# The last batch's gate values stored as rows in the tail, weight loads behind the first two gathers, and gate gathers ahead of the last token gathers

## The chip, the cores and the metric

The kernel runs on 1 core of one Trainium2 chip. The metric is the device time of one execution in microseconds (us). Before the change three executions took 1396.22 to 1399.36 us, with a median of 1397.73 us. One more execution was profiled; all rows below come from it.

## The reference

The program is an attention without softmax whose output is multiplied by `u`, followed by a mixture of experts with a capacity. B = 8, S = 2496, D = 256, 8 experts, capacity 80:

```python
scores = (1.0 / S) * np.matmul(z, z.transpose(0, 2, 1))
x = u * np.matmul(np.maximum(scores, 0.0) ** 2, v)      # rows of all batches: N = 19968
logits = x @ w_gate
expert_idx = np.argmax(logits, axis=1)
gate_w = softmax(logits)[expert_idx]                    # of the chosen expert
out = zeros((N, D))
for e in range(E):
    tok_idx = tokens of expert e, at most `capacity` of them (largest gate_w)
    h = np.maximum(x[tok_idx] @ w1[e], 0.0)             # 256 -> 1024
    out[tok_idx] = gate_w[tok_idx, None] * (h @ w2[e])  # 1024 -> 256
```

## The kernel before

**Main part.** Eight batches with five column chunks of 512 each (the last has 448) go through TensorE (PE): scores, square, attention, then a chunk of `x` is made, stored in the DRAM tensor `xs` (one row a token), and multiplied with the gate's weights. After each batch the logits become gate values, one column of `gall` per 128 tokens. For the batches up to the seventh these values go to the DRAM tensor `gd` by `gate_store` (L651): PE transposes the columns, VectorE (DVE) copies the result, SyncE (SP) writes rows of 512 bytes. For the last batch they go by `gate_put` (L661): SP writes straight from `gall` with a swapped access pattern, which makes every value a piece of 4 bytes. The last batch is done in two parts, 16 columns (four chunks) in `finished_late` and 4 columns in `ahead`.

**Tail.** `ahead` (L1616) computes the 8 experts, one unit of 80 tokens each. All engines have their order written out by hand there, so an engine does its instructions in the order of the program, and what waits holds up all that stands behind it on that engine. The steps of a unit i:

- `token(i)` (L1471): DVE finds the row numbers `tok` of the unit's tokens, GpSimd (POOL) gathers these rows of `xs` into `xg` by an indirect DMA.
- `whole(i)`: DVE turns `xg` into `xf`; `ffn_x`, `ffn_xl`: PE transposes it, ScalarE (ACT) and DVE make a high and a low part of it (`xTh`, `xTl`).
- `ffn1(i, part)`: PE, 6 matmuls into `hp`, ACT applies the Relu; `ffn_h(i, half)`: PE transposes `h` (`tp`), ACT and DVE split it into `hTh` and `hTl`; `ffn2(i)`: PE, 24 matmuls into `op`.
- `target(i)` (L1491): POOL gathers the gate values `gt` from `gd`, DVE works out the output rows `slo`; `result(i)`: ACT multiplies `op` by `gt` into `ob`, POOL scatters `ob` to `out`.

For the units 2 to 7 the row numbers come from tables for all of them at once: `many_blocks`, `many_rows`, `many_within` on DVE, `many_pe` and `many_fetch` on PE and ACT.

**Weights.** Each expert's w1 and w2 come as 4 pieces of 512 KB (`loads`, L774; SP issues them) into 6 places, and `split(n)` turns n of them into a high part (ACT) and a low part (DVE) and asks for one further piece each. Experts 0 and 1 are done in the main part; expert 2 is loaded whole, and its low parts are made by `half_lo` in the tail. `loads(n, after)` lets POOL write one element of each place first (L754), so that the load comes behind what POOL does before it.

Of the kernel before, what the change touches and what calls it, by code (L numbers as in the profile page):

```python
# [8 lines left out]
F32 = mybir.dt.float32  # L9
# [3 lines left out]
U16 = mybir.dt.uint16  # L13
AF = mybir.ActivationFunctionType
ALU = mybir.AluOpType
AX = mybir.AxisListType
# [3 lines left out]
P = 128  # L20
# [6 lines left out]
def attn_moe_kernel(ctx, tc, zT, uT, v, wg, w1, w2, out, seq, cap):  # L27
# [5 lines left out]
    nc = tc.nc  # L33
    V = nc.vector
# [588 lines left out]
    def gate_near(b, q0):  # L623

        _, d, ex, near = gate_t[b, q0]
        ci = n_gates[0]
        n_gates[0] += 1
        V.tensor_scalar(out=near, in0=d, scalar1=-2.0 ** -25, scalar2=0.0, op0=ALU.is_gt,
                        op1=ALU.add, accum_out=nsum[:, ci:ci + 1])
        V.scalar_tensor_tensor(out=ex, in0=ex, scalar=1.0, in1=near, op0=ALU.min, op1=ALU.max)  # L630
# [27 lines left out]
        V.tensor_copy(out=gs[:nt], in_=gt[:nt, :P])  # L658
        nc.sync.dma_start(out=gd[col:col + nt], in_=gs[:nt])

    def gate_put(b, q0):  # L661

        col, nt = gcol.pop((b, q0))
        nc.sync.dma_start(out=gd[col:col + nt].rearrange("c p -> p c"), in_=gall[:, col:col + nt])


    def count(k0, k1):
        n = (k1 - k0) * E
        tp = ps_m.tile([P, CH], F32, tag="m", name=f"tp_{k0}")
# [103 lines left out]
    def loads(n, after=None):  # L773
        n = min(n, NR - len(ready))  # L774
        for p in pieces[:n]:
            ready.append((p, load_raw(*p, after)))
        del pieces[:n]
# [11 lines left out]
    def half_lo(eng=V):  # L789
        rv, hv, lv = halves.pop(0)  # L790
        eng.tensor_tensor(out=lv, in0=rv, in1=hv, op=ALU.subtract)
# [74 lines left out]
    SPLITS = dict(zip([(qb, 0), (qb, 2), (qb, 5), (qb, 8), (qz, 2), (qz, 4), (qz, 7), (qz, 9)], early))  # L866

    RAW = {(qz, 0): (2, 1), (qz, 5): (2, 2)}
    WARM = 6
    steps = [(b, qc, r) for b in range(B) for qc in range(NQ) for r in range(NP)]  # L870
    ET = mybir.EngineType
    v_raw, z_raw, w_raw = {}, {}, {}
# [60 lines left out]
    def finished_late(b, qc, r):  # L933

        kb = b * BPB
        part = kb, kb + BPB - 2
        if r == 0:
            chunk_store(b, qc)
        elif r == 1:
            chunk_hi(b, qc)  # L940
            chunk_rest(b, qc)
        elif r == 2:
            chunk_mid(b, qc)
        elif r == 3:
            chunk_lo(b, qc)
            chunk_store2(b, qc)
        elif r == 4:
            chunk_logits(b, qc)
            chunk_sum(b, qc)
        elif r == 5:  # L950
            gate_top(b, 0, NQ - 1)
        elif r == 6:
            gate(b, 0, NQ - 1)
        elif r == 7:
            gate_put(b, 0)
        elif r == 8:
            count(*part)
            up_to(*part)
            half()
# [9 lines left out]
    if True:  # L969
# [41 lines left out]
        def whole(i):  # L1011
            begin(i)
            middle(i)
            low(i)
            turn(i)
# [140 lines left out]
        for kk, c in ((3, 0), (2, 0), (3, 1), (1, 0), (2, 1), (1, 1)):  # L1156
            attend(*prev, NT - kk, [c])
            if kk == 1:
                chunk_x_last(*prev, c)
        loads(2)  # L1160
        halves_hi(2)
        chunk_logits_last(*prev)
        chunk_rows_last(*prev)
# [176 lines left out]
    def steps_of(own, tl, tw, ps_t, ps_h):  # L1340
# [64 lines left out]
        def many_blocks():  # L1405
            rk = rank[:, 0, es].rearrange("p (e o) -> p e o", o=1).broadcast_to([P, E - 2, NBLK])
            tt(le_g[1][:, :, 1:], incl[:, es], rk, ALU.is_le)
            V.tensor_reduce(out=small["cnt"][:, es], in_=le_g[1][:, :, 1:], axis=AX.X, op=ALU.add)
            bo = tl.tile([P, E - 2, NBLK], F32, name="bo_rest")
            tt(bo, le_g[1][:, :, :NBLK], le_g[1][:, :, 1:], ALU.subtract)  # L1410
            x_t["bo"] = bo

        def many_rows():
            le = le_g[1][:, :, 1:]
# [58 lines left out]
        def token(i):  # L1473

            ns = num(i)
            _, _, wr, rin, base = sl[i]
            lw = tw.tile([P, 2 * P], BF16, tag="lw", name=f"lw_{i}{own}", bufs=1)
            j = col("j", i)
            V.tensor_scalar(out=lw[:ns], in0=wr[:ns], scalar1=rin[:ns], scalar2=0.0,
                            op0=ALU.is_le, op1=ALU.add, accum_out=j[:ns])  # L1480
            tok = col("tok", i, I32)
            ts(tok[:ns], j[:ns], base[:ns], ALU.add, float(NTOK - 1), ALU.min)
            xg = tw.tile([P, 2, D], U16, tag="xg", name=f"xg_{i}{own}", bufs=8)
            nc.gpsimd.indirect_dma_start(  # L1484
                out=xg[:ns].rearrange("p h w -> p (h w)"), out_offset=None,
                in_=xs.rearrange("(n h) w -> n (h w)", h=2),
                in_offset=bass.IndirectOffsetOnAxis(ap=tok[:ns], axis=0))
            xg_t[i] = [xg, tok, j]
# [86 lines left out]
        def result(i):  # L1575
            ns, op = num(i), o_t.pop(i)
            _, gt, slo = xg_t.pop(i)
            ob = tw.tile([P, D], F32, tag="ob", name=f"ob_{i}{own}")
            nc.scalar.activation(out=ob[:ns], in_=op[:ns, :D], func=AF.Copy,
                                 scale=gt[:ns])  # L1580
            nc.gpsimd.indirect_dma_start(  # L1581
                out=out[:, :], out_offset=bass.IndirectOffsetOnAxis(ap=slo[:ns], axis=0),
                in_=ob[:ns], in_offset=None, bounds_check=NTOK - 1, oob_is_err=False)
# [6 lines left out]
        def flags_end():  # L1590
            flags2(ps_t, "t")

        early_steps = (ps_t, ps_h, places_, one_block, one_within, (many_blocks, many_rows, many_within,
                       many_pe, many_fetch), pe_block, pe_fetch, warm_up, flags_v, flags_end, x_t, sl)
        return early_steps, (empty, block, fetch, within, token, target, whole, ffn_x, ffn_xl, ffn1,
                             ffn_h, ffn2, result)
# [25 lines left out]
    def ahead(early_steps, steps):  # L1622

        ET = mybir.EngineType
        (ps_t, ps_h, places_, one_block, one_within, many, pe_block, pe_fetch, warm_up,
         flags_v, flags_end, x_t, sl) = early_steps
        many_blocks, many_rows, many_within, many_pe, many_fetch = many
        empty, _, _, _, token, target, whole, ffn_x, ffn_xl, ffn1, ffn_h, ffn2, result = steps

        def split(n):  # L1630

            for _ in range(n):
                if ready:
                    p, raw = ready.pop(0)
                    split_w(*p, raw, V)
                    loads(1)

        def spread(i):
            if i < NU:
                whole(i)  # L1640

        def from_table(i):
            pe_fetch(i)
            sl[i][2] = x_t.pop(i)

        PL = nc.gpsimd
        with tc.manual_schedule(engines={ET.Pool}):
            places_()
            one_block(0)
            pe_block(0)  # L1650
            one_block(1)
            pe_block(1)
            tot_last(B * BPB - 2, B * BPB)
            from_table(0)
            one_within(0)
            token(0)
            from_table(1)
            one_within(1)
            token(1)
            halves_hi(2)  # L1660
            for e in range(2, E, 2):
                pe_tables(e, ps_h, "h")
            gate_near(B - 1, NQ - 1)
            gcol[B - 1, NQ - 1] = gate_sum(B - 1, NQ - 1, NQ)
            gate_put(B - 1, NQ - 1)
            loads(2, PL)
            warm_up(WARM)
            many_blocks()
            whole(0)
            ffn_x(0)  # L1670
            many_rows()
            ffn_xl(0)
            many_within()
            many_pe()
            whole(1)
            ffn1(0, 0)
            many_fetch()
            ffn_x(1)
            ffn_xl(1)
            token(2)  # L1680
            token(3)
            ffn1(0, 1)
            ffn_h(0, 0)
            ffn1(1, 0)
            ffn_h(0, 1)
            empty()
            whole(2)
            ffn_x(2)
            ffn_xl(2)
            for _ in range(4):  # L1690
                half_lo()
            ffn1(1, 1)
            target(0)
            split(1)
            token(4)
            spread(3)
            split(1)
            target(1)
            ffn2(0)
            for i in range(2, NU):  # L1700
                ffn_h(i - 1, 0)
                ffn_h(i - 1, 1)
                ffn1(i, 0)
                if i + 1 < NU:
                    ffn_x(i + 1)
                    ffn_xl(i + 1)
                if i == 3:
                    result(0)
                    result(1)
                if i + 3 < NU:  # L1710
                    token(i + 3)
                split(2)
                ffn1(i, 1)
                spread(i + 2)
                split(2)
                target(i)
                if i == NU - 1:
                    ffn_h(i, 0)
                ffn2(i - 1)
                if i > 2:  # L1720
                    result(i - 1)
                if i == 5:
                    flags_v()
                if i == 6:
                    flags_end()
            ffn_h(NU - 1, 1)
            ffn2(NU - 1)
            result(NU - 1)
# [44 lines left out]
```

## Time and profile before

| what | value |
|---|---|
| median of 3 executions | 1397.73 us (1396.22 to 1399.36) |
| the profiled execution | 1396.5 us, its span 1394.8 us |
| granted TensorE clock over the span | 0.989 |
| PE busy | 1350.3 us (97%) |
| DVE, ACT busy | 1070.9 us (77%), 1027.0 us (74%) |
| POOL busy | 34.6 us (2%) |

The main part fills about 1294 us of the span and keeps PE busy nearly throughout. The change touches only the last 110 us: the end of the main part, the preparation of the tail's tables up to 1307.2 us, and the eight units from 1322.0 us on. A row of the timeline has start, duration, engine, line, operation, tiles and, in brackets, how long the engine was idle before it and what ended that. "SPq" rows are the issuing of DMAs by SP: their duration is that of the issue, not of the transfer.

### The profile page before, as it was taken

To read this page: it belongs to the slowest core of one execution; us is meant where nothing else is said; L and a number is where in the kernel's file an instruction comes from. 1 tells how busy PE (TensorE), PEld (TensorE's weight loads), DVE (VectorE), ACT (ScalarE), POOL (GpSimd) and SP (SyncE) were. 2 spreads that over 40 slices of the span, in tenths; PEclk is the share of its full clock that TensorE was granted. 3 is DMA by queue.
4 is the path that set the end of the run, shared out by engine and by line. 5 is a ranking of instruction groups with operands and counts; after the bars stand their busy time and mean duration, and the time that the engine had idled before them with its cause. 6 is when DMAs were issued, how large, how long until landed. Compare 5 with 4: busy or idle time off the path is not lost. (4 is left out here: it accounts for less than half of the span.)

```text
span 1394.8 us, 30057 instructions
## 1 busy us (share of the span) xinstructions
PE 1350.3 (97%) x12047; PEld 1128.1 (81%) x12047; DVE 1070.9 (77%) x1557; ACT 1027.0 (74%) x1322; POOL 34.6 (2%) x44
## 2 busy tenths in 40 slices
PE   8999999999999999999999999999999999999486
PEld 5888888898878888898887888888887988778365
DVE  6877787787877787877878777877877877877474
ACT  6877797777876697677876687777877778776364
POOL 0000000000000000000000000000000000000034
PEclk9999999999999999999999999999999999999699
DMA  5699969997979969997879969998789977999552
GB/s 175 195 262 282 249 183 257 244 249 211 252 188 280 244 175 248 256 268 220 234 194 261 270 156 249 260 276 209 228 230 221 278 196 219 239 288 274 149 169 85
DMA packets 262676, 318.09 MB, mean 228 GB/s; under 512 B 96558, under 2 KB 187650, under 8 KB 252290
## 3 DMA queue, kind: packets, MB, share of 16 engines
q1 hardware_dynamic: 261506, 314.79, 84.7%
q8 instruction: 96, 1.57, 0.5%
q0 software_dynamic: 1024, 1.31, 0.3%
q14 instruction: 50, 0.41, 0.1%
HBM read 153.23 MB, written 126.05 MB: 200 GB/s over the span
## 5 line engine op out<-in xcount | busy, mean ns | idle before, releaser
L441 PE MATMUL acc<-ah,vt 64*128 64x512 f32 (+1 forms) x6004 | 835.8, 387 | 1.5 <-DVE vt L159 0.9
L441 PEld LDWEIGHTS acc<-ah,vt 64*128 64x128 f32 x6004 | 606.0, 184 | 102.5 <-DVE vt L159 2.3
L441 PE MATMUL acc<-al,vt 64*128 64x512 f32 (+1 forms) x3002 | 488.3, 386 | 0.3 <-DVE al L55 0.3
L55 DVE TENSOR_TENSOR al<-a,ah 128x1024 fp32r<-128x1024 f32 (+1 forms) x240 | 291.3, 1214 | 171.3 <-ACT ah L370 130.9
L364 ACT ACTIVATE a<-s 128x512 f32<-128x512 f32 (+1 forms) x480 | 258.4, 590 | 178.2 <-PE s L361 175.7
L441 PEld LDWEIGHTS acc<-al,vt 64*128 64x128 f32 x3002 | 315.7, 184 | 51.4 <-DVE al L55 1.4
L367 ACT ACTIVATE a<-a 128x1024 f32<-128x1024 f32 (+1 forms) x240 | 253.1, 1055 | 7.4
L55 DVE TENSOR_TENSOR al<-blk,ah 128x1024 fp32r<-128x1024 f32 x160 | 193.7, 1211 | 48.8 <-PE acc L441 27.5
L342 ACT CAST ah<-blk 128x1024 fp32r<-128x1024 f32 x160 | 167.1, 1047 | 84.0 <-PE acc L441 77.7
L297 DVE STREAM_TRANSPOSE x<-a 128x512 f32<-128x512 f32 x320 | 207.5, 686 | 0.0
L370 ACT CAST ah<-a 128x1024 fp32r<-128x1024 f32 x160 | 168.0, 1050 | 5.1
L361 PE MATMUL s<-zm,zs 64*128 64x512 f32 x960 | 147.1, 394 | 1.6 <-DVE zs L121 1.2
L361 PEld LDWEIGHTS s<-zm,zs 64*128 64x128 f32 x960 | 97.4, 184 | 20.4 <-ACT a L364 1.8
L361 PE MATMUL s<-zm 64*128 64x512 f32 x480 | 74.1, 398 | 1.9 <-ACT a L364 1.9
L375 DVE CAST ah<-a 128x1024 fp32r<-128x1024 f32 (+1 forms) x80 | 53.8, 672 | 26.5 <-ACT a L367 26.3
L361 PEld LDWEIGHTS s<-zm 64*128 64x128 f32 x480 | 47.9, 184 | 11.0 <-ACT a L364 2.7
L159 DVE TENSOR_TENSOR vt<-vraw,vt 128x1024 fp32r<-128x1024 f32 (+1 forms) x40 | 46.1, 1153 | 6.9 <-ACT vt L108 6.1
L55 DVE TENSOR_TENSOR xb<-xf,xb 128x1024 bf16<-128x1024 f32 (+1 forms) x38 | 45.3, 1192 | 0.2
L55 DVE TENSOR_TENSOR xf<-xf,xb 128x1024 f32<-128x1024 f32 (+1 forms) x38 | 44.9, 1182 | 0.2
L108 ACT CAST vt<-vraw 128x1024 fp32r<-128x1024 f32 (+3 forms) x56 | 44.9, 829 | 0.0
L491 ACT CAST xb<-xf 128x1024 bf16<-128x1024 f32 (+1 forms) x39 | 39.7, 1018 | 5.0 <-DVE xf L55 2.8
L1484 POOL DMA_INDIRECT xg<-xs,tok x8 | 10.2, 1280 | 1334.0 <-DMA gd<-gall 1316.7
(173 smaller groups left out, 741.7 us busy)
## 6 DMA issues: line engine op xcount, KB each, us to landing
y<-x SPq DMA_DIRECT2D x80, 1024.0 KB, 9.1
blk<-y SPq DMA_DIRECT2D x320, 256.0 KB, 6.7
out<-idle SPq DMA_DIRECT2D x40, 512.0 KB, 3.7
vraw<-v SPq DMA_DIRECT2D x32, 512.0 KB, 7.6
zm<-zs SPq DMA_DIRECT2D x128, 128.0 KB, 6.2
ut<-uT SPq DMA_DIRECT2D x32, 512.0 KB, 6.9
xs<-xq SPq DMA_DIRECT2D x32, 512.0 KB, 7.9
wraw<-w SPq DMA_DIRECT2D x28, 512.0 KB, 6.6
```

Of the source, the lines that this page charges most:

```text
L55: V.tensor_tensor(out=o, in0=a, in1=b, op=op)
L108: eng.copy(out=o, in_=i)
L159: e1.tensor_tensor(out=vt[:, :nf, 1], in0=raw[:, :nf], in1=vt[:, :nf, 0], op=ALU.subtract)
L297: V.transpose(out=x[:, :, :, t].rearrange("p n k s -> p k n s"), in_=a)
L342: nc.scalar.copy(out=natural(ah), in_=src)
L361: nc.tensor.matmul(s, zk, zm[rows, :, y].rearrange("p h k t -> p k h t"), start=i == 0, stop=i == 2)
L364: nc.scalar.activation(out=a[:, h, :nq], in_=s[:, :nq], func=AF.Relu)
L367: nc.scalar.activation(out=a[:, :, :nq], in_=a[:, :, :nq], func=AF.Square)
L370: nc.scalar.copy(out=st["ah"][:, :, :nq], in_=a[:, :, :nq])
L375: V.tensor_copy(out=ah[:, :, :nq], in_=a[:, :, :nq])
L441: ins = nc.tensor.matmul(acc[c], vt, a[rows, k % 2, :nq], start=p == pairs[0] and group == 0 and i == 0, stop=p == pairs[-1] and group == ...
L491: nc.scalar.copy(out=xb[:, 0], in_=xf)
```

## The change

1. Both `gate_put` of the last batch go away. The 4 columns' gate values are computed later (DVE, after the first half of unit 0's `ffn_h`), and all 20 columns go to `gd` by `gate_store` there: a transpose on PE, a copy on DVE, one DMA of 20 rows of 512 bytes.
2. Of the six weight pieces that are requested before the tail's units, two instead of four are requested ahead of the last store to `xs`; four instead of two are requested behind the first two gathers.
3. `many_pe` comes ahead of `whole(0)`; the counting reduction (`many_counts`) is taken out of `many_blocks` and comes behind unit 0's transposes. WARM, the number of matmuls that only keep PE running there, is 3 instead of 6.
4. The gathers `xg` of the units 4 to 7 and the gate gathers `gt` of the units 0 to 3 are all issued before the loop over the units 2 to 7, the `gt` of 0 to 3 ahead of the `xg` of 6 and 7.
5. In the loop `result` comes one unit later and `ob` has 3 places instead of 2, `xg` 6 instead of 8.

```diff
-    def gate_put(b, q0):
-        col, nt = gcol.pop((b, q0))
-        nc.sync.dma_start(out=gd[col:col + nt].rearrange("c p -> p c"), in_=gall[:, col:col + nt])
...
-    WARM = 6
+    WARM = 3
...
             gate(b, 0, NQ - 1)
-        elif r == 7:
-            gate_put(b, 0)
...
-        loads(2)
         halves_hi(2)
         chunk_logits_last(*prev)
...
-            xg = tw.tile([P, 2, D], U16, tag="xg", name=f"xg_{i}{own}", bufs=8)
+            xg = tw.tile([P, 2, D], U16, tag="xg", name=f"xg_{i}{own}", bufs=6)
...
-            ob = tw.tile([P, D], F32, tag="ob", name=f"ob_{i}{own}")
+            ob = tw.tile([P, D], F32, tag="ob", name=f"ob_{i}{own}", bufs=3)
...
-            gate_near(B - 1, NQ - 1)
-            gcol[B - 1, NQ - 1] = gate_sum(B - 1, NQ - 1, NQ)
-            gate_put(B - 1, NQ - 1)
-            loads(2, PL)
+            loads(4, PL)
             warm_up(WARM)
             many_blocks()
+            many_pe()
             whole(0)
             ffn_x(0)
+            many_counts()
+            many_fetch()
+            ffn_xl(0)
             many_rows()
-            ffn_xl(0)
             many_within()
-            many_pe()
+            token(2)
+            ffn1(0, 0)
+            ffn1(0, 1)
             whole(1)
-            ffn1(0, 0)
-            many_fetch()
             ffn_x(1)
             ffn_xl(1)
-            token(2)
             token(3)
-            ffn1(0, 1)
             ffn_h(0, 0)
             ffn1(1, 0)
+            gate_near(B - 1, NQ - 1)
+            gcol[B - 1, 0] = gcol[B - 1, 0][0], gcol[B - 1, 0][1] + gate_sum(B - 1, NQ - 1, NQ)[1]
+            gate_store(B - 1, 0, ps_t, "t")
+            token(4)
+            token(5)
+            empty()
+            for i in range(4):
+                target(i)
             ffn_h(0, 1)
-            empty()
             whole(2)
+            half_lo()
+            half_lo()
+            ffn1(1, 1)
             ffn_x(2)
             ffn_xl(2)
-            for _ in range(4):
-                half_lo()
-            ffn1(1, 1)
-            target(0)
+            half_lo()
+            half_lo()
+            token(6)
             split(1)
-            token(4)
             spread(3)
             split(1)
-            target(1)
+            token(7)
             ffn2(0)
             for i in range(2, NU):
...
-                if i == 3:
-                    result(0)
-                    result(1)
-                if i + 3 < NU:
-                    token(i + 3)
+                if i > 2:
+                    result(i - 2)
                 split(2)
                 ffn1(i, 1)
                 spread(i + 2)
                 split(2)
-                target(i)
+                if i == 2:
+                    result(0)
+                if i > 3:
+                    target(i)
                 if i == NU - 1:
                     ffn_h(i, 0)
                 ffn2(i - 1)
-                if i > 2:
-                    result(i - 1)
+                if i == 4:
+                    flags_v()
                 if i == 5:
-                    flags_v()
-                if i == 6:
                     flags_end()
+            result(NU - 2)
             ffn_h(NU - 1, 1)
```

On SP, at the end of the main part, stand before: the two writes of gate values (`gd<-gall`), the weight pieces (`wraw`) and the two stores of the last chunk of `x` (`xs<-xq`; 128x3x512 is its first 384 tokens).

```order
L664 DMA gd<-gall 128x16x1
L756 DMA wraw_1_0_17942<-w 128x1024
L756 DMA wraw_1_1_17944<-w 128x1024
L756 DMA wraw_2_0_17968<-w 128x4x256
L756 DMA wraw_2_1_17970<-w 128x4x256
L550 DMA xs<-xq_4_17986 128x3x512
L552 DMA xs<-xq_4_17986 64x512
L664 DMA gd<-gall 128x4x1
L756 DMA wraw_1_0_18151<-w 128x1024
L756 DMA wraw_1_1_18154<-w 128x1024
```

With the change the same place of SP reads:

```order
L750 DMA wraw_1_0_17941<-w 128x1024
L750 DMA wraw_1_1_17943<-w 128x1024
L550 DMA xs<-xq_4_17981 128x3x512
L552 DMA xs<-xq_4_17981 64x512
L750 DMA wraw_2_0_18135<-w 128x4x256
L750 DMA wraw_2_1_18138<-w 128x4x256
L750 DMA wraw_1_0_18141<-w 128x1024
L750 DMA wraw_1_1_18144<-w 128x1024
L659 DMA gd<-gs_0_18262 20x128
```

Two weight pieces and both writes of single gate values no longer stand around the stores to `xs`; the pieces stand behind them, and one write of 20 rows behind those.

On POOL, from the first gather on, stand before (`xg` token rows, `gt` gate values, `out` results, the MEMSETs are those that hold back the weight loads):

```order
L1484 DMA xg_18095<-xs,tok_18093 80x512
L1484 DMA xg_18110<-xs,tok_18108 80x512
L754 MEMSET wraw_1_0_18151 128x1
L754 MEMSET wraw_1_1_18154 128x1
L1484 DMA xg_18228<-xs,tok_18226 80x512
L1484 DMA xg_18235<-xs,tok_18233 80x512
L1497 DMA gt_18293<-gd,tok_18093 80x1
L1484 DMA xg_18308<-xs,tok_18306 80x512
L1497 DMA gt_18316<-gd,tok_18108 80x1
L1484 DMA xg_18382<-xs,tok_18380 80x512
L1497 DMA gt_18414<-gd,tok_18226 80x1
L1581 DMA out<-ob_18475,slo_18295 20480x256
```

With the change POOL has, behind the first two gathers and four MEMSETs:

```order
L1477 DMA xg_18197<-xs,tok_18195 80x512
L1477 DMA xg_18230<-xs,tok_18228 80x512
L1477 DMA xg_18270<-xs,tok_18268 80x512
L1477 DMA xg_18277<-xs,tok_18275 80x512
L1490 DMA gt_18281<-gd,tok_18088 80x1
L1490 DMA gt_18285<-gd,tok_18103 80x1
L1490 DMA gt_18289<-gd,tok_18195 80x1
L1490 DMA gt_18293<-gd,tok_18228 80x1
L1477 DMA xg_18330<-xs,tok_18328 80x512
L1477 DMA xg_18349<-xs,tok_18347 80x512
L1574 DMA out<-ob_18438,slo_18283 20480x256
```

All eight `xg` now stand ahead of the first scatter to `out`; before, the `xg` of the units 6 and 7 stood behind three and four of them.

## Rows read from the trace of the kernel before

**Rows 1.** Windows over the tail: from:to, length, each engine's busy us, PEclk, DMA share, GB/s
```profile
core 0: us, PE busy (x) PEld busy (x) DVE busy (x) ACT busy (x) POOL busy (x), PEclk, DMA share, GB/s
1312.20:1319.30 7.10, 0.00 (x0) 0.00 (x0) 0.00 (x0) 0.00 (x0) 0.01 (x1) 0.50 0.00 0
...
1322.00:1342.10 20.10, 17.08 (x94) 12.62 (x95) 13.88 (x33) 9.54 (x20) 4.05 (x4) 0.82 0.23 77
1342.10:1349.00 6.90, 6.90 (x51) 5.72 (x49) 6.86 (x14) 5.93 (x12) 5.99 (x4) 1.00 0.75 233
```

**Rows 2.** Waits from 1305 us on: who waited for whom, us in total, times, longest
```profile
POOL xg L1484 <- DMA gd<-gall: 1316.7, 1, 1316.7
...
DVE xf L1508 <- DMA xg<-xs,tok: 17.4, 4, 14.8
...
ACT ob L1579 <- DMA out<-ob,slo: 2.9, 1, 2.9
```

**Rows 3.** Timeline of SP at the end of the main part
```profile
1290.64 0.62 SPq L664 DMA_DIRECT2D gd<-gall  x1
1291.36 10.01 SPq L756 DMA_DIRECT2D wraw<-w  x4
1301.46 2.42 SPq L550 DMA_DIRECT2D xs<-xq  x1
...
1306.44 0.54 SPq L664 DMA_DIRECT2D gd<-gall  x1
```

**Rows 4.** Timeline of POOL, its first gather
```profile
1319.29 1.09 POOL L1484 DMA_INDIRECT xg<-xs,tok  x1 [1316.73 <-DMA gd<-gall]
```

**Rows 5.** Timeline of ACT, the copy that the store to xs waits for
```profile
1297.67 1.93 ACT L547 COPY xq<-xp 128x1024 uint16<-128x1024 uint16 x2 [1.24 <-PE xp L545]
```

**Rows 6.** DMA issues on the page: KB each, median us from issue to landing
```profile
out<-idle SPq DMA_DIRECT2D x40, 512.0 KB, 3.7
...
xs<-xq SPq DMA_DIRECT2D x32, 512.0 KB, 7.9
```

**Rows 7.** Chain of waits near the end: start, us, what
```profile
1384.62 3.17 DMA out<-ob,slo
```

**Rows 8.** Timeline of POOL, its last scatter
```profile
1388.69 0.93 POOL L1581 DMA_INDIRECT out<-ob,slo  x1 [3.12 <-DVEq L1733]
```

**Rows 9.** Timeline of DVE, from the first row numbers to the loop
```profile
1302.52 0.21 DVE L61 TENSOR_SCALAR tok<-j,base_all 80x1 int32<-80x1 f32 x1
...
1303.91 0.17 DVE L628 TENSOR_SCALAR_CACHE_REDUCE fw<-d 128x32 f32<-128x32 f32 x1
...
1305.34 0.63 DVE L55 TENSOR_TENSOR scratch<-incl,rank 128x480 f32<-128x480 f32 x1
...
1306.57 0.65 DVE L55 TENSOR_TENSOR bo_rest<-scratch 128x480 f32<-128x480 f32 x1
1322.02 0.45 DVE L1508 COPY xf<-xg 80x512 uint16<-80x512 uint16 x1 [14.80 <-DMA xg<-xs,tok]
...
1342.08 0.88 DVE L55 TENSOR_TENSOR hTl<-tp,hTh 128x320 fp32r<-128x320 f32 x2
```

**Rows 10.** Groups of DVE instructions over the span: busy us, mean ns of one
```profile
L1479 DVE TENSOR_SCALAR_CACHE_REDUCE lw<-ws,rin_all 80x256 bf16<-80x256 bf16 x6 | 2.8, 468 | 0.0
...
L61 DVE TENSOR_SCALAR slo<-j,base_all,none 80x1 int32<-80x1 f32 x8 | 2.1, 265 | 0.0
...
L658 DVE COPY gs<-gt 20x128 f32<-20x128 f32 x7 | 1.9, 271 | 0.0
```

**Rows 11.** Timeline of PE, transposes that open a unit of the loop
```profile
1345.38 0.72 PE L1556 MATMUL tp<-ident,h 80*128 80x80 f32 x8
...
1351.99 0.72 PE L1556 MATMUL tp<-ident,h 80*128 80x80 f32 x8
...
1377.21 0.75 PE L1556 MATMUL tp<-ident,h 80*128 80x80 f32 x8
```

**Rows 12.** Windows: a stretch behind a pause of PE in the tail
```profile
1332.00:1336.00 4.00, 3.17 (x10) 2.15 (x11) 2.77 (x5) 0.36 (x2) 0.91 (x1) 0.58 0.08 21
```

More of the change, by code (lines that the diff above doesn't have):

```diff
@@ L1407, in many_blocks @@
             tt(le_g[1][:, :, 1:], incl[:, es], rk, ALU.is_le)
-            V.tensor_reduce(out=small["cnt"][:, es], in_=le_g[1][:, :, 1:], axis=AX.X, op=ALU.add)
             bo = tl.tile([P, E - 2, NBLK], F32, name="bo_rest")
@@ L1411, in many_blocks, with many_counts @@
             x_t["bo"] = bo
+        def many_counts():
+            V.tensor_reduce(out=small["cnt"][:, es], in_=le_g[1][:, :, 1:], axis=AX.X, op=ALU.add)
         def many_rows():
@@ L1591, in flags_end @@
             flags2(ps_t, "t")
-        early_steps = (ps_t, ps_h, places_, one_block, one_within, (many_blocks, many_rows, many_within,
+        early_steps = (ps_t, ps_h, places_, one_block, one_within, (many_blocks, many_counts, many_rows, many_within,
                        many_pe, many_fetch), pe_block, pe_fetch, warm_up, flags_v, flags_end, x_t, sl)
@@ L1626, in ahead @@
          flags_v, flags_end, x_t, sl) = early_steps
-        many_blocks, many_rows, many_within, many_pe, many_fetch = many
+        many_blocks, many_counts, many_rows, many_within, many_pe, many_fetch = many
         empty, _, _, _, token, target, whole, ffn_x, ffn_xl, ffn1, ffn_h, ffn2, result = steps
```

## The prediction

> **What bounds the kernel now.** I read the page first: PE is busy for 97% of the span, so the main part is PE's, and the change does not touch it. What the change touches is the tail, so I read the tail by windows, then the waits, then the timelines of SP, POOL, DVE and PE there.
>
> The windows show a hole. From 1312.2 to 1319.3 us nothing runs at all: PE, DVE and ACT are at 0.00, and the DMA share is 0.00 too [rows 1]. DVE in fact has no work from the end of its table work (1306.57 + 0.65 = 1307.2) until 1322.02, when the first gathered tokens arrive [rows 9]. The waits name what ended it: the first gather `xg` on POOL waited for the DMA `gd<-gall`, and the first `xf` waited 14.8 us for that gather [rows 2]. The gather reads `xs`, not `gd`; but SP issued the last store to `xs` at 1301.46 and the second write of gate values right behind it at 1306.44 [rows 3], and POOL started its gather only at 1319.29 [rows 4]. The store itself came late: ACT had its data ready at 1297.67 + 1.93 = 1299.6 [rows 5], but SP was still issuing four weight pieces, which took it 10.01 us behind the first write of gate values [rows 3]. So I read the hole as the work of the two writes in pieces of 4 bytes: the first slows the weight loads ahead of the store, the second is in flight together with the store and holds up its completion.
>
> From 1322.02 on there are two stages. Until the loop starts (DVE's `hTl` of unit 1 at 1342.08 [rows 9]) nothing is full: of 20.10 us DVE is busy 13.88 and PE 17.08, the latter partly at the lower clock (mean 0.82) [rows 1]. In the loop PE sets the pace at first, busy 6.90 of 6.90 us from 1342.1 on [rows 1]: the unit from 1345.38 to 1351.99 takes 6.61 us. Then three units take 1377.21 - 1351.99 = 25.22 us, 8.41 each [rows 11].
>
> **Term 1, the first gather comes earlier.** Without the first write and with two weight pieces instead of four ahead of it, SP can issue the store at 1299.6, when ACT is done. How long it then takes to land no row shows for a quiet queue. From below: SP's writes of zeros, 512 KB each to DRAM, land after 3.7 us (median); from above: the stores to `xs` in the main part, 512 KB among much other traffic, after 7.9 us [rows 6]. This store has 384 KB and a queue that is nearly empty, so I take the nearer, 3.7: landed at 1303.3. POOL starts 0.9 us behind what releases it: the last scatter at 1388.69 [rows 8], when the one before had landed at 1384.62 + 3.17 = 1387.79 [rows 7]. The gather then starts at 1304.2; its row numbers are there at 1302.52 + 0.21 = 1302.7 [rows 9], so they are not late. `xf` follows 1322.02 - 1319.29 = 2.73 us behind [rows 4, 9]: 1306.9 instead of 1322.02, a gain of 15.1 us. With 7.9 us it is 1311.1 and a gain of 10.9. DVE's table work that stays ahead of `xf` begins where the gate work stood, at 1303.9, and takes 0.63 + 0.65 us, so it ends at 1305.2 [rows 9] and is hidden behind the gather. So are `many_pe` and the 3 warming matmuls on PE; taking the other 3 away is worth nothing, since PE waited anyway.
>
> The four weight pieces now come behind the second gather, at about 1306.5. Were they to land in two pairs of 7.9 us each [rows 6], they would be there by 1322.3. The first two pieces, which are still loaded ahead of the store, are split near the end of the stage up to the loop, and the four only in the loop. So I cost this at nothing; it would cost as much as they came late. The second gather shares the DMA engines with them; it is needed only behind unit 0's table rows and `token(2)`.
>
> **Term 2, up to the loop.** DVE took 1342.08 - 1322.02 = 20.1 us from the first `xf` to the loop, with 13.88 us of work and so 6.2 us of waits [rows 1, 9]. The change puts more on DVE there: the counting reduction, (1306.57 - 1305.34) - 0.63 = 0.6; the gate work, 1305.34 - 1303.91 = 1.4 [rows 9]; the copy `gs`, 0.27; three more `token` (units 5 to 7) at 0.47 for `lw` and 0.21 for `tok`, 2.0; two more `slo` at 0.27, 0.5 [rows 9, 10]. Together 4.8, so 18.7 us of work. Its waits should shrink, as there is always other work between an order to PE and its use, except at two places: `xTl` of unit 1 now stands behind both halves of unit 0's `ffn1` on PE, and `gs` waits for its transpose. I put these at 1.8 us, under a third of the waits of now. The bounds are 0 and the 6.2 of now. So 20.5 us (18.7 to 24.9): a loss of 0.4 (a gain of 1.4 to a loss of 4.8).
>
> The wait that is added: the first `gt` waits for the new write to `gd`, and behind it on POOL stand three `gt` and the `xg` of the units 6 and 7. Those two are needed in the loop's third and fourth unit, some 15 us later. They are early enough even if the write takes as long as the slowest of rows 6.
>
> **Term 3, the loop.** The three slow units took 25.22 - 3 x 6.61 = 5.4 us more than the pace of the one before [rows 11]. The waits name two causes. ACT waited 2.9 us for a scatter to free `ob`, and DVE waited 17.4 - 14.8 = 2.6 us in three more waits for an `xg` [rows 2]. The third place for `ob` and the early `xg` take both away. What is late next is DVE: it was busy 6.86 of 6.90 us from 1342.1 on [rows 1], of which a `token` (0.7) and a `slo` (0.27) go, so about 5.9 a unit are left, close under PE's 6.61. I take back two thirds of the 5.4, 3.5 (bounds 0 and 5.4). The end, from the last `ffn2` over two scatters that wait for one another to the end of the span, is unchanged.
>
> **Sum.** 15.1 - 0.4 + 3.5 = 18.2 us. The profiled execution had a span of 1394.8 and took 1396.5 us, 1.7 more; minus 18.2 it is 1378.3. The median of the runs is 1.2 above the profiled one, 1397.73; that gives 1379.5 us.
>
> **Rivals.**
>
> *The store's completion is slow by itself.* The gap from the last packet at 1312.2 to the release at 1319.29 - 0.9 = 1318.4 would be the store's own 6.2 us, which no removal takes away. For it: nothing but the store and the small write was in flight, and the trace names the write only as the last to land. Against it: SP's other writes land 3.7 us after issue, transfer included [rows 6]. It is the upper bound of term 1: 10.9 - 0.4 + 3.5 = 14.0, or 1383.7 us.
> The Trainium skill's page "DMA: Bandwidth & Descriptors", section "Queues, rings and completion order", says that a DMA's completion mark lands after all earlier writes of the same DMA engine; by that, a write issued later should not hold up the store's mark. This rule speaks for this rival; rows 2 put the end of the wait on the later write.
>
> *The loop gains nothing.* As PE's stalls go, DVE and the splits of the weights hold the pace near 8.4 us. For it: DVE was full where PE was [rows 1]. Against it: that unit took 6.61 us with a `token` on DVE that is now gone. 15.1 - 0.4 = 14.7, or 1383.0 us.
>
> *PE stays at the lower clock.* After a pause of PE the granted clock fell to half: 0.58 on average from 1332 to 1336 [rows 12], 0.50 while PE stood still [rows 1]. DVE's added work gives PE more pauses before the loop. If PE's work there ran at the 1.2 GHz level, the stage would take its upper bound, and one unit of the loop might cost another 6.61: 15.1 - 4.8 + 3.5 - 6.6 = 7.2, or 1390.5 us.
> The Trainium skill's page "TensorE: Matmul & The Clock Gate", section "HAM oscillation — how this bites in real kernels", describes kernels whose short bursts between waits all start at the low clock. Rows 12 show one such burst in this tail; the loop's granted clock of 1.00 shows none [rows 1].
>
> *The same, slower than before.* Its place is the loop: at half the clock a unit costs 6.6 us more. To eat 18.2 us and 2.8 more, over three of the six units have to run so. That is the point from which it decides; for it speaks only that PE then has pauses, against it the clock of 1.00 in the loop now [rows 1]. With four such units it would be 1379.5 + 4 x 6.6 = 1405.9 us.
>
> *The wait stays.* The first gather waits for something else that lands at 1318. Then only terms 2 and 3 are left, 3.1 us: 1394.6 us. For it speaks only that the trace names the last of several releasers.
>
> **How the numbers follow.** Forecast 0.55 (1376 to 1382), slow completion 0.15 (1383.7), no gain in the loop 0.15 (1383), low clock 0.08 (1390.5), wait stays 0.04 (1394.6), slower 0.03 (1405.9). Measurements of this kernel tell 0.2%, 2.8 us, from no change. Faster: 0.55 + 0.15 + 0.15 + 0.08 and half of the fifth, 0.95; same 0.02; slower 0.03. The lowest time takes the best of each term, 15.1 + 1.4 + 5.4 = 21.9, 1375.8; the range starts a little under it, 1375, as the store might land sooner. Its upper end takes the worst of each term, 10.9 - 4.8 + 0 = 6.1, 1391.6; I end it at 1390, since all three together are unlikely.
>
> **What would show it.** Right: POOL's first gather starts at 1304 to 1306, `xf` of unit 0 at about 1307, no stretch over 3 us in which all engines stand, `hTl` of unit 1 at about 1327.5, and units of 6.6 to 7.3 us in the loop with no wait of ACT for a scatter. Wrong: a first gather behind 1308 (term 1), DVE waits over 4 us before the loop or a mean clock under 0.8 there (term 2), units over 7.5 us (term 3). A time above 1392 would say that the gather still waits.

## The result and the profile after

The changed kernel took 1380.24 us (median of 4 runs, 1379.5 to 1380.79) beside 1398.55 us for the kernel before (4 runs, 1396.22 to 1400.14): a ratio of 0.987, 95% interval 0.9853 to 0.9887. The prediction was 1379.5 us.

The two profiled executions had spans of 1394.8 and 1377.8 us. Their main parts end 2.0 us apart: ACT's copy for the last store starts at 1297.67 before [rows 5] and here at 1299.71. The change takes only one small write and two weight loads of SP away ahead of this copy, and the 2.0 us are not their doing: in the fourteen profiles below the copy starts at 1297.67 to 1300.08 us, and in the three that have that write at 1297.67, 1299.99 and 1299.11. So I measure all times of the tail from the start of that copy (line 547).

Timeline of ACT after, the same copy:

```profile
1299.71 1.93 ACT L547 COPY xq<-xp 128x1024 uint16<-128x1024 uint16 x2 [1.30 <-PE xp L545]
```

Timeline of SP after, where [rows 3] were:

```profile
1301.67 0.38 SPq L550 DMA_DIRECT2D xs<-xq  x1
1302.09 0.50 SPq L552 DMA_DIRECT2D xs<-xq  x1
1308.31 1.96 SPq L750 DMA_DIRECT2D wraw<-w  x4
```

The store is issued the moment ACT is done (1301.64). Its issue takes 0.38 us instead of 2.42, and four weight pieces take 1.96 us instead of 10.01 [rows 3]. DMA issues after, from 1301.6 to 1309 us (KB each, median us to landing):

```profile
xs<-xq SPq DMA_DIRECT2D x1, 384.0 KB, 2.7
...
xg<-xs,tok POOLq DMA_INDIRECT x2, 2.6
```

Timeline of POOL after, from the first gather on:

```profile
1305.86 1.09 POOL L1477 DMA_INDIRECT xg<-xs,tok  x1 [1303.31 <-DVE lw L1472]
...
1322.43 5.48 POOL L1490 DMA_INDIRECT gt<-gd,tok  x1 [0.30 <-issue]
...
1332.67 5.03 POOL L1477 DMA_INDIRECT xg<-xs,tok  x1 [0.30 <-issue]
```

The first gather comes 6.15 us behind the copy instead of 21.62 [rows 4, 5], and what it waits for is named DVE, no longer a DMA. Timeline of DVE after, where [rows 9] were:

```profile
1304.56 0.21 DVE L61 TENSOR_SCALAR tok<-j,base_all 80x1 int32<-80x1 f32 x1
...
1308.56 0.45 DVE L1501 COPY xf<-xg 80x512 uint16<-80x512 uint16 x1 [1.27 <-DMA xg<-xs,tok]
1309.96 0.32 DVE L55 TENSOR_TENSOR xTl<-xp,xTh 128x160 fp32r<-128x160 f32 x1 [0.41 <-ACT xTh L1513]
...
1315.73 0.33 DVE L55 TENSOR_TENSOR xTl<-xp,xTh 128x160 fp32r<-128x160 f32 x1 [2.78 <-ACT xTh L1513]
...
1330.94 0.88 DVE L55 TENSOR_TENSOR hTl<-tp,hTh 128x320 fp32r<-128x320 f32 x2
```

`xf` waits 1.27 us instead of 14.80. The new longest wait ahead of the loop is 2.78 us, for unit 1's transposed rows. Windows of the tail after (columns as in [rows 1]):

```profile
1305.00:1312.00 7.00, 6.66 (x33) 5.10 (x33) 5.06 (x15) 4.69 (x9) 2.22 (x6) 0.50 0.43 128
1312.00:1316.00 4.00, 3.56 (x18) 2.17 (x16) 1.18 (x6) 1.66 (x4) 0.92 (x1) 0.86 0.95 362
...
1308.60:1330.90 22.30, 18.40 (x95) 13.22 (x93) 18.14 (x53) 10.26 (x20) 11.49 (x7) 0.82 0.36 120
```

There is no window of zeros any more. But from 1305 to 1312 PE runs at a granted clock of 0.50 (1.2 GHz), though it is busy 6.66 of 7.00 us. Timeline of PE after, the transposes that open a unit (compare [rows 11]):

```profile
1327.06 0.72 PE L1549 MATMUL tp<-ident,h 80*128 80x80 f32 x8
1334.12 0.72 PE L1549 MATMUL tp<-ident,h 80*128 80x80 f32 x8
1340.42 0.72 PE L1549 MATMUL tp<-ident,h 80*128 80x80 f32 x8
1346.69 0.72 PE L1549 MATMUL tp<-ident,h 80*128 80x80 f32 x8
1353.35 0.75 PE L1549 MATMUL tp<-ident,h 80*128 80x80 f32 x8
```

The units take 7.06 us, then 6.30, 6.27 and 6.66. The next one is slower, 7.73: ACT waits in it for gate values:

```profile
1358.26 0.47 ACT L1572 ACTIVATE ob<-op,gt 80x256 f32<-80x256 f32 x1 [0.89 <-DMA gt<-gd,tok]
```

### The profile page after: what moved, and what is told of

It is laid out like the page before. It is cut to its first block, busy times and chain, and to the rows that moved or that the text cites. A ratio compares the mean times of both kernels' runs of the same rounds, so it can differ in the third digit from the quotient of the medians.

```text
span 1377.8 us, 30051 instructions
## 1 busy us (share of the span) xinstructions
PE 1352.2 (98%) x12044; PEld 1127.6 (82%) x12045; DVE 1071.2 (78%) x1558; ACT 1027.6 (75%) x1322; POOL 37.5 (3%) x46
```

## The experiments

The table has, from each profile, the time since the start of the copy of line 547: to POOL's first gather, to the first `xf`, to the loop (DVE's `hTl` of unit 1), to the end of the span; then the loop alone.

| kernel | gather | first rows | loop | end | loop alone |
|---|---|---|---|---|---|
| before | 21.6 | 24.4 | 44.4 | 97.1 | 52.7 |
| before, no first write | 6.5 | 9.5 | 36.2 | 90.3 | 54.2 |
| before, no second write | 15.1 | 17.8 | 38.2 | 92.6 | 54.4 |
| before, neither | 6.1 | 9.5 | 28.7 | 81.8 | 53.1 |
| after | 6.2 | 8.9 | 31.2 | 78.1 | 46.9 |
| after, a write ahead of the store | 12.4 | 15.1 | 37.6 | 84.6 | 47.0 |
| after, a write behind the store | 6.2 | 13.6 | 36.8 | 83.9 | 47.1 |
| after, four weight pieces ahead | 6.4 | 9.4 | 31.3 | 82.3 | 50.9 |
| after, last `token` in the loop | 6.1 | 8.9 | 29.5 | 89.4 | 59.9 |
| after, `ob` with 2 places | 6.1 | 8.8 | 31.5 | 81.6 | 50.1 |
| after, WARM 6 | 6.2 | 8.9 | 30.8 | 79.1 | 48.3 |
| after, 2 warming matmuls earlier | 6.4 | 9.1 | 31.5 | 79.8 | 48.3 |
| after, DVE's wait filled | 6.2 | 8.9 | 30.0 | 77.0 | 47.0 |
| after, filled and WARM 6 | 6.1 | 8.8 | 29.7 | 78.5 | 48.8 |

**The two writes taken out of the kernel before, one at a time and together.** The values that a removed write carried go to `gd` as rows in the tail.

```diff
-        elif r == 7:
-            gate_put(b, 0)
...
             ffn_h(0, 1)
+            gate_store(B - 1, 0, ps_t, "t")
             empty()
```

> Kernel before, but the 16-column write of gate values in 4-byte pieces is taken away; these columns go by rows in the tail, ahead of unit 0's gate gather. The other write (4 columns) and the four weight pieces ahead of the store to xs stay. Theory (the 4-byte writes delay the store): the store leaves as soon as ACT is done and lands before the second write starts, so POOL's first gather starts 7 to 9 us after the start of ACT's copy to xq (before: 21.6, with the change: 6.2) and the time falls by 12 to 15 us, to 1384 to 1387. Rival (the two weight pieces more ahead of the store are what delays it): the first gather stays over 15 us behind the copy, time 1392 or more. Rival (only the second write matters): no gain over 3 us.

Without the first: 1392.12 us, ratio 0.9957 (0.9943 to 0.9971). A miss: 5 us above the expected range. Timeline of POOL in it:

```profile
1306.61 1.09 POOL L1482 DMA_INDIRECT xg<-xs,tok  x1 [1304.05 <-ACT scratch L859]
1308.01 1.20 POOL L1482 DMA_INDIRECT xg<-xs,tok  x1 [0.31 <-DVE gall L642]
```

Timeline of SP, the second write, and of DVE, the second unit's rows:

```profile
1307.92 0.37 SPq L664 DMA_DIRECT2D gd<-gall  x1
```

```profile
1318.20 0.45 DVE L1506 COPY xf<-xg 80x512 uint16<-80x512 uint16 x1 [6.54 <-DMA xg<-xs,tok]
```

The store and the first gather are on time now. The write is issued as the second gather starts, and it is that gather whose rows come late: DVE waits 6.54 us for them.

```diff
-            gate_put(B - 1, NQ - 1)
...
             ffn_h(0, 1)
+            gate_store(B - 1, NQ - 1, ps_t, "t")
             empty()
```

> Kernel before, but the 4-column write of gate values in 4-byte pieces is taken away; these columns go by rows in the tail. The 16-column write stays. Theory: the store still leaves late behind the first write and the weights (its packets end some 14 us behind the start of ACT's copy), but lands 1 to 3 us after that instead of 6: first gather 16 to 18 us behind the copy, a gain of 4 to 6 us, 1393 to 1395. Rival (the store's completion is slow by itself, 6 us): no gain, 1398.

Without the second: 1393.09 us, 0.9961 (0.9946 to 0.9977), as the theory said, though the first gather comes 15.1 us behind the copy, a little sooner than the 16 to 18 expected. Timeline of SP and of POOL in it:

```profile
1303.23 2.94 SPq L550 DMA_DIRECT2D xs<-xq  x1
```

```profile
1315.07 1.09 POOL L1484 DMA_INDIRECT xg<-xs,tok  x1 [1312.51 <-issue]
```

The first write still slows the store, whose issue takes 2.94 us; from the store's issue to the gather it is 11.8 us, and 17.8 with both writes [rows 3, 4].

> Kernel before, but both writes in 4-byte pieces are taken away; all 20 columns go by rows in the tail. The weights' order and the tail's order stay as before. Theory: as without the first write or up to 2 us better: first gather 6 to 8 us behind ACT's copy, time 1383 to 1386; the rest of the change's gain (about 4 to 6 us in the loop) is not there. Rival (weights' order makes the gain): 1392 or more.

Without either (both edits, one `gate_store` for all 20 columns): 1383.93 us, 0.9904 (0.9887 to 0.992), as the theory said. Timeline of POOL in it:

```profile
1305.90 1.09 POOL L1482 DMA_INDIRECT xg<-xs,tok  x1 [1303.34 <-DVE lw L1477]
```

The first gather comes 6.1 us behind the copy, as in the changed kernel. The gain is 13.1 us, where one write alone gives 4.9 or 4.0. In the profiles the end comes 15.3 us sooner, with one alone 6.8 or 4.5: either write by itself keeps more than half of the loss.

**A write put back into the changed kernel.** Nobody reads what it writes. First 16 columns ahead of the store:

```diff
+        elif r == 7:
+            col, nt = gcol[b, 0]
+            nc.sync.dma_start(out=gx[col:col + nt].rearrange("c p -> p c"), in_=gall[:, col:col + nt])
```

> Changed kernel with one more DMA that nothing reads: 16 columns of gate values in 4-byte pieces to a spare DRAM tensor, where the first such write stood before the change (ahead of two weight pieces and the store to xs). Theory: it blocks the queue for about 13 us, the two weight pieces and the store come out behind it; first gather 9 to 12 us behind the start of ACT's copy to xq instead of 6.2, time 1383 to 1386. Rival (only the weights' order or the tail's order matters): 1380, as the changed kernel.

1385.78 us, 0.9915 (0.9898 to 0.9931). Timeline of POOL in it:

```profile
1311.55 1.10 POOL L1481 DMA_INDIRECT xg<-xs,tok  x1 [1308.99 <-issue]
```

The gather starts 12.4 us behind the copy instead of 6.2. Then 4 columns right behind the store:

```diff
         chunk_rows_last(*prev)
+        nc.sync.dma_start(out=gx[:4].rearrange("c p -> p c"), in_=gall[:, :4])
```

> Changed kernel with one more DMA that nothing reads: 4 columns (512 pieces of 4 bytes) to a spare DRAM tensor, issued by SP right behind the two stores to xs. Theory (a write in small pieces that is in flight together with the store holds up the store's completion): first gather 3 to 6 us later, time 1383 to 1386. Rival (the Trainium skill's rule in DMA: Bandwidth & Descriptors, Queues, rings and completion order: a later write of the same engine does not hold up an earlier mark): the store lands as before, 1380.

1386.04 us, 0.9915 (0.9899 to 0.9932). The time is at the upper end of the expected range, but not for the reason I gave. Timelines of SP, POOL and DVE in it:

```profile
1301.03 0.38 SPq L551 DMA_DIRECT2D xs<-xq  x1
...
1302.01 0.58 SPq L1156 DMA_DIRECT2D gx<-gall  x1
```

```profile
1305.29 1.66 POOL L1479 DMA_INDIRECT xg<-xs,tok  x1 [1302.73 <-DVE lw L1474]
```

```profile
1312.63 0.45 DVE L1503 COPY xf<-xg 80x512 uint16<-80x512 uint16 x1 [5.96 <-DMA xg<-xs,tok]
```

DMA issues in it, from 1301 to 1312.6 us:

```profile
xg<-xs,tok POOLq DMA_INDIRECT x2, 7.0
gx<-gall SPq DMA_DIRECT2D x1, 2.0 KB, 10.4
```

The gather starts as early as without the write, so the store was complete: the write behind it did not hold it up. What it holds up is what is issued behind it: the gathers take 7.0 us instead of 2.6 to landing, and the four weight pieces behind them 10.7 instead of 4.0. The Trainium skill, page "DMA: Bandwidth & Descriptors", section "Queues, rings and completion order", says that a DMA's mark lands after all earlier writes of its DMA engine; by that it need not wait for later ones, and this run agrees, as to the store. Where the first write has made the store late, the second does add 6.0 us between its issue and the gather (17.8 against 11.8 above). It is not the moving of data that is late there: before, the last packet of any transfer ends by 1312.4 and the gather starts 6.9 us behind it [rows 1, 4]; without the second write the packets end by 1313.6 and the gather starts 1.5 us behind them. The rule alone gives no such delay, and what holds back the release between the last packet and the gather stays open. The small write has such a gap of its own: in this run 560 packets under 512 bytes are recorded from 1301 to 1304.2 us and no packet at all from there to 1307.6, yet the write lands only at 1302.01 + 10.4 = 1312.4.

**Weights.** Four pieces ahead of the store and two behind, as before:

```diff
+        loads(2)
         halves_hi(2)
...
-            loads(4, PL)
+            loads(2, PL)
```

> Changed kernel, but with four weight pieces ahead of the store to xs and two behind the first gathers, as before the change. Theory: the four pieces move while ACT still makes the copy, so the store is at most 2 us later: 1380 to 1382. Rival (the weights' order makes the gain): 1388 or more.

1379.89 us (1377.34 to 1382.08), 0.9867 (0.9847 to 0.9886): no difference is seen, so the move of the pieces costs and brings nothing that can be measured here. The profiled execution took 1382.08 us, and its loop is the longest of those that the edits leave alone.

**The row numbers of units 5 to 7 back in the loop.**

```diff
             token(4)
-            token(5)
...
                 if i > 2:
                     result(i - 2)
+                if i + 3 < NU:
+                    token(i + 3)
```

> Changed kernel, but the row numbers and gathers of the units 5, 6 and 7 are back in the loop, three units ahead, as before the change. Theory (early gathers take away stalls of the loop): DVE has 2 us less before the loop, but waits for xg in the loop again and carries a token a unit: 1381 to 1384. Rival (the third place of ob makes the loop faster, the early gathers do nothing): 1378.5 to 1380.

1389.24 us, 0.9926 (0.9909 to 0.9943): 5 us above the expected range. Timeline of POOL and of DVE, and windows in it (columns as above):

```profile
1336.35 0.91 POOL L1477 DMA_INDIRECT xg<-xs,tok  x1 [0.30 <-DVE xTl L55]
```

```profile
1342.17 0.45 DVE L1501 COPY xf<-xg 80x512 uint16<-80x512 uint16 x1 [2.99 <-DMA xg<-xs,tok]
```

```profile
1337.00:1342.50 5.50, 3.53 (x28) 2.72 (x26) 2.51 (x3) 3.98 (x7) 1.58 (x2) 1.00 1.02 351
1342.50:1349.00 6.50, 6.08 (x33) 5.13 (x34) 6.26 (x11) 4.92 (x7) 2.28 (x2) 0.74 0.69 232
```

The gather of unit 5 now comes behind the gate gathers and beside weight loads (DMA share 1.02); DVE waits 2.99 us for it, PE stands, and the next stretch runs at a clock of 0.74. DVE waits 6.5 us in all for three gathers in this loop, and the loop takes 13 us more in this profile (by the medians the kernel loses 9.0). I had priced the waits alone, without what PE loses behind them. The stage ahead of the loop got shorter by 1.8 us, about what three `token` cost on DVE. (One count given with the change is too high: before it, the gathers of the units 6 and 7 stand behind two and three scatters on POOL, not three and four.)

**`ob` with 2 places.**

```diff
-            ob = tw.tile([P, D], F32, tag="ob", name=f"ob_{i}{own}", bufs=3)
+            ob = tw.tile([P, D], F32, tag="ob", name=f"ob_{i}{own}")
```

> Changed kernel with two places for ob instead of three. Theory: ACT waits again for a scatter to land in one or two units, 1381 to 1384. Rival (one unit later for result already gives it the time): 1380, no wait of ACT for a scatter.

1382.24 us, 0.9881 (0.9865 to 0.9898), as expected, but the interval overlaps that of the changed kernel, and 50.1 us for the loop is inside the spread of the other rows. The waits of ACT in the loop show the wait of before [rows 2] back again:

```profile
ACT ob L1572 <- DMA out<-ob,slo: 3.1, 1, 3.1
```

**What the stage ahead of the loop is short of.** More warming matmuls behind the tables (`WARM = 6`):

> The changed kernel with WARM 6 instead of 3. In the profile of the changed kernel PE's granted clock is 0.50 from 1300 to about 1312.9, and DVE waits 2.8 us for unit 1's transposed rows behind unit 0's first matmuls. Theory A (the lost 2 us ahead of the loop come from matmuls at the half clock, and more work of PE ahead of them raises the clock sooner): the clock rises by 1311, the wait shrinks by 1 us or more, but three more matmuls of about 0.5 us stand ahead of the transposes of the table rows, so the time is 1379 to 1381, no more than 0.1% from the changed kernel. Theory B (PE's clock does not follow from the warming matmuls there): the three matmuls only delay, 1.5 us, 1381 to 1383.

1378.59 us, 0.9866 (0.9849 to 0.9882), a little under both expectations. Windows in it (columns as above):

```profile
1305.00:1308.00 3.00, 2.83 (x11) 1.47 (x11) 1.29 (x3) 0.56 (x1) 1.12 (x5) 0.51 0.35 83
1308.00:1312.00 4.00, 3.49 (x22) 2.49 (x21) 2.85 (x9) 2.88 (x6) 0.10 (x1) 1.00 1.03 347
```

The clock is at its full level from 1308 on, 10.3 us behind the copy instead of some 13. Unit 1's wait falls from 2.78 to 1.30 us, unit 0's grows from 0.41 to 1.38, and the stage takes 21.9 us instead of 22.4. Two of these matmuls in PE's pause before the tables instead:

```diff
             one_block(0)
+            warm_up(2)
             pe_block(0)
```

> The changed kernel with two more warming matmuls, not behind the tables but in the pause of 1.2 us that PE has ahead of the first block's transposes (1301.65 to 1302.84 in the profile of the changed kernel). They stand ahead of nothing that is ready. Theory A (the clock rises sooner when that pause is filled): the granted clock rises 1.5 to 3 us sooner, the wait for unit 1's transposed rows falls under 2 us, 1378 to 1379.5. Theory B (the clock is not set by that pause): no change, 1380 to 1381, and the clock still rises at about 1312.9.

1378.23 us, 0.986 (0.9843 to 0.9876). By the time it would be theory A, but by its windows B: the mean clock is still 0.50 from 1310 to 1312 and 0.58 from 1312 to 1314, and the stage takes 22.3 us. So 2 us between kernels that were timed apart say nothing, and in this group I go by the stages. Then DVE's own order:

```diff
             whole(1)
+            token(3)
+            gate_near(B - 1, NQ - 1)
+            gcol[B - 1, 0] = gcol[B - 1, 0][0], gcol[B - 1, 0][1] + gate_sum(B - 1, NQ - 1, NQ)[1]
             ffn_x(1)
             ffn_xl(1)
-            token(3)
             ffn_h(0, 0)
             ffn1(1, 0)
-            gate_near(B - 1, NQ - 1)
-            gcol[B - 1, 0] = gcol[B - 1, 0][0], gcol[B - 1, 0][1] + gate_sum(B - 1, NQ - 1, NQ)[1]
```

> The changed kernel with unit 3's row numbers and the gate work of the last four columns ahead of unit 1's low part on DVE, instead of behind it, so that DVE has about 2.1 us of work where it now waits 2.8 us for PE. Theory A (the wait is DVE's own and delays the loop, as DVE is what the stage before the loop runs on): loop 1.5 to 2.2 us earlier, 1377.5 to 1379. Theory B (PE at the half clock is the bound, DVE's order does not matter): unit 1's matmuls and the first transposes come as late as before, 1380 to 1381, and the wait is only moved to a later place of DVE.

1378.26 us, 0.986 (0.9844 to 0.9877). Timeline of DVE in it:

```profile
1315.38 0.32 DVE L55 TENSOR_TENSOR xTl<-xp,xTh 128x160 fp32r<-128x160 f32 x1 [0.73 <-ACT xTh L1513]
...
1317.30 0.28 DVE L658 COPY gs<-gt 20x128 f32<-20x128 f32 x1 [1.10 <-PE gt L656]
...
1329.42 0.87 DVE L55 TENSOR_TENSOR hTl<-tp,hTh 128x320 fp32r<-128x320 f32 x2
```

The wait is 0.73 us, 0.7 of what it lost comes back at `gs`, and the stage takes 21.1 us: 1.3 gained, a little less than the 1.5 to 2.2 expected. Both together:

> The changed kernel with both: DVE's work of 2.1 us in the place of its wait, and WARM 6, which made PE's granted clock rise some 3 us sooner. Theory A (the two gains add, as one fills the wait and the other shortens what is waited for): the stage from unit 0's first rows to the loop takes 20.5 to 21 us instead of 22.4, 1377 to 1378.5. Theory B (what is left of the wait is gone already, and the three matmuls delay unit 0's rows by 1 us): 21.1 us or more for the stage, 1378 to 1380. Either way the difference to the changed kernel is about what a measurement of this kernel can tell.

1378.18 us, 0.9855 (0.9839 to 0.9872); the stage takes 20.9 us, as theory A said. It is faster than the kernel before; from the changed one its interval doesn't separate it. The loop took 48.8 us in its profile, so the 1.5 us did not show at the end of that profile (78.5 us, against 78.1 for the changed kernel).

## Why the prediction held, step by step

**What bounds the tail.** Right in the main: the hole was the work of the two writes in pieces of 4 bytes. Taking them out alone brings 13.1 of the 18.3 us. What failed is the part played by the second: "the second is in flight together with the store and holds up its completion". By itself it leaves the store alone and holds up the gather that comes next, 6.54 and 5.96 us. Behind the first it does lengthen the wait for the store, by 6.0 us; how it does so was not found. For the sum it made no difference, as both go.

**Term 1** (15.1): from the copy to the first `xf` it is 8.85 us instead of 24.35 [rows 5, 9], 15.5. The store was issued when I said and landed in 2.7 us, where I took 3.7 from the writes of zeros [rows 6]. Of that 1 us only 0.4 was gained: the gather now waits for its row numbers, which I had put at 1302.7 in the time of before; they come 5.1 us behind the copy in both. So the rival of a slow completion is out.

**Term 2** (a loss of 0.4): a loss of 2.3, 22.4 us instead of 20.1. The work on DVE was right, 18.14 us against 18.7; the term that was mis-sized is the waits, put at 1.8 and in fact 4.2 (22.30 - 18.14), just over the 4 us that I had set as the sign that this term is wrong. Most of it stands at one of the two places that I had named, unit 1's `xTl` behind both halves of unit 0's `ffn1`: 2.78 us. `gs` waits only 0.37, and the other 1.0 stands at places that I had put at nothing. The wait of unit 1's `xTl` was there before, too, so it shrank less than I took; timeline of DVE before:

```profile
1328.49 0.32 DVE L55 TENSOR_TENSOR xTl<-xp,xTh 128x160 fp32r<-128x160 f32 x1 [4.06 <-ACT xTh L1520]
```

I had not priced that unit 0's first matmuls, which stand ahead of it on PE, run at half the clock (before, 0.50 from 1322 to 1325 us; after, up to about 1313). That is not the rival of the lower clock: the stage's mean clock is 0.82 both times [rows 1]. A clock that rises 3 us sooner gave 0.5 us, filling the wait 1.3, both together 1.5 of the lost 1.9; the rest is open.

**Term 3** (3.5): too small. The loop is 5.9 us shorter in this profile, above my bound of 5.4. One and the same loop varies from profile to profile, so one pair is not enough: the four profiles with the loop of before have it at 52.7 to 54.4 us, mean 53.6, and the eight with the changed loop at 46.9 to 50.9, mean 48.0. The gain is about 5.6 us, and as the two groups do not overlap, the rival of no gain in the loop is out. What failed is the floor of 6.61 us a unit, read from a single unit that still had a `token` on DVE: two units take 6.30 and 6.27 now. I also named two causes where the waits of before [rows 2] show a third, ACT's wait for gate values:

```profile
ACT ob L1579 <- DMA gt<-gd,tok: 2.8, 2, 1.8
```

That late gathers cost the loop dearly was shown; that ACT's wait of 3.1 us for a scatter comes back with 2 places for `ob` too, but not what it costs. What is late next is `gt` of unit 4, in the unit of 7.73 us, which is over my sign of 7.5: ACT waits 0.89 us for it here, 2.8 us in the last experiment.

**The rest.** The weight pieces cost nothing, as costed. The wait that stays, and the slower case (three or more units at half the clock), did not come: from 1334.12 to 1346.69 two units take 6.29 us each.

**The sum**: 15.5 - 2.3 + 5.9 = 19.1 against 18.2, less the 2.0 us by which the main part of this execution was longer: 17.0, the difference of the spans. The medians differ by 18.3. The two terms that were off, +2.4 and -1.9, nearly cancel: that the sum came out within 1 us of the measured time is luck in part.

Without the writes, the kernel before is at a ratio of 0.9904, the changed one at 0.987, and the two intervals just touch. Parts 2 to 5 of the change bring 3.7 us by the two medians and by the two profiles, 5.2 by the two gains (18.3 - 13.1). By the stages of these profiles that is 0.6 us up to the first rows, a loss of 3.1 up to the loop and a gain of 6.3 in it.

## What to carry to other kernels

A transfer that moves almost nothing (2 KB) can cost more than 512 KB when it is cut into pieces of 4 bytes (here 10.4 us to land against 4.0): look for it in front of whatever waits for a DMA, whether or not the trace names it, and write rows instead. Two such causes can hide each other: taking out one brought a third of what both bring, so test them together too. When the hole in front of a stage closes, read the clock at which the next stage now starts, and move work that an engine has anyway into the wait that appears.

## What was not expected of the hardware

- The write of 2 KB in 512 pieces took 10.4 us to land behind a store on an otherwise quiet queue, 8 us behind the last of its packets in the trace, and gathers issued after it took 7.0 instead of 2.6 us, though they go by another queue.
- An indirect gather that takes POOL 0.91 us took 5.48 and 5.03 us at two places after (above), in nearly the same length in each run with that order. DVE split weights there. The Trainium skill, page "SBUF — State Buffer", section "Who interferes with whom", says that DVE's operations with two inputs from SBUF contend with GpSimd's reads, and also reports a probe in which such operations did not stall a DMA. The trace has the two side by side, but it has a scatter beside such a split, too, that took 1.27 us (at 1339.23), and no run took one of them away: the cause is open.
- PE's granted clock stayed at 0.50 from 1305 to 1312 although PE was busy 6.66 of 7.00 us; three more warming matmuls behind the tables brought the full level about 3 us sooner, two ahead of the tables did not.
